# Attention on one core: the product with v one and a half key steps behind the scores, in pieces of half, whole, half

## The chip, the cores and the metric

The kernel runs on one core of a Trainium2 chip. A core has a matrix engine (TensorE, PE in the profile; its loads of the stationary operand are shown as PEld), a vector engine (VectorE, DVE), a scalar engine for activations (ScalarE, ACT), a general engine (GpSimd, POOL) and an engine that issues transfers (SyncE, SP). Each works through its own list of instructions in order; semaphores make one wait for another. The metric is the device time in microseconds (us); three runs of the kernel before the change gave 2307.34, 2310.35 and 2310.27, median 2310.27.

## The reference

One transformer block on 2048 tokens of width 576, in float32: modulation by a condition vector, attention with 32 heads of width 18 that share one key and one value head, and a channel MLP of width 4608, each behind a LayerNorm.

```
h = layernorm(x) * (1 + ca) + sa
q = h @ wq   (32 heads of 18);  k = h @ wk;  v = h @ wv   (one head of 18)
p = softmax(q k^T * 18**-0.5);  o = p v
x = x + ga * (o @ wo)
h = layernorm(x) * (1 + cb) + sb
x = x + gb * (gelu(layernorm(h) @ w1 + b1) @ w2 + b2)
```

## The kernel before

The program has three stages: projections (to about 138 us), attention (to about 1431 us), MLP. The order of instructions on each engine is the order in which the Python code issues them; there is no scheduler.

Attention goes through 32 **quads**. A quad is one block of 512 queries and four heads. For each quad the 2048 keys are taken in 16 **key steps** of 128. In one key step the scores of the four heads are four matmuls (`st_mm`, L790), each of 64 rows of the array, with the keys stationary and 512 queries streaming; heads of group g = 0 use the upper half of the array's rows and those of g = 1 the lower half, so that two neighbouring matmuls of different g run at the same time. Each result fills one of the four PSUM banks called psB, and ScalarE turns it into exponentials (L792), one instruction a bank, in a quarter of an SBUF tile P; three such tiles exist. The product with v (`pv_mm`, L779) takes a whole tile P as moving operand, with v (32 columns) stationary, in four column groups for the four heads, and adds all 16 key steps up in the single PSUM bank psC. A call for all 512 queries is a whole, for 256 a half.

The rows of the queries carry the negated maximum of their scores, so the scores come out with it subtracted. These maxima are computed one quad and two loop steps ahead: in every loop step, for two lots of 128 queries (g = 0 and 1), the scores against all 2048 keys are formed again in pieces of 512 keys. They are `m` (`mx_mm`, L313, into one of three banks psM, reduced by VectorE, L812), six a loop step; `x` (L800, a psB bank), the difference of two key blocks, of which ScalarE takes the relu (L803); and `r` (L313, psM), which VectorE combines with that relu (L810), so that eight pieces cost seven VectorE results.

A **loop step** `d` (there are 256, eight a quad) covers two key steps and follows a written list of tokens, MIX: `s0`/`s1` a score matmul of group 0 or 1, `m0`/`m1`, `x1`, `r1` as above, `H` a half product and `P` a whole one. The last ten steps have no maxima to compute and follow PLAIN. Behind a finished key step `between(n, kc)` issues what is due by the number kc of the key step: at 12 the last reductions of the maxima (L346, L347), at 13 their transpose on TensorE (L351), ScalarE's and VectorE's halves of the negated value (L353, L354) and four transfers into the queries' rows; one piece of every finished quad's normalisation (`post_quad`: copy of psC by ScalarE, L610; at 1 a transpose of 32x32 blocks on VectorE, L614; at 2 a reciprocal, L617; at 4 a second transpose, L622; at 5 another copy); at odd kc one piece of other work (first weights, then for each block of 512 queries the product with wo, L591, and for the first two blocks the second LayerNorm, with L138 to L143 on VectorE); and on GpSimd the preparation of the MLP's weights.

Of the kernel before, what the change touches and what calls it, by code (L numbers as in the profile page):

```python
# [14 lines left out]
S, D, H, DH, F = 2048, 576, 32, 18, 4608  # L15
# [5 lines left out]
NQT = NB * NQ  # L21
# [9 lines left out]
def block_kernel(ctx: ExitStack, tc, x, wqkv, wo, w1, b1, w2, b2, c, wmod, ident_in, out):  # L31
# [20 lines left out]
    def psC(): return PS["t"].tile([128, 512], F32, name="psC", bufs=1)  # L52

    open_ps("1", 3)
    def big(): return per.tile([128, 10, 512], F32R, name="big", bufs=3)
# [244 lines left out]
    def load_q(n):  # L300
        tb, qd = divmod(n, NQ)
        if n not in QST:
            new_q(n)
        q = QST[n]
        for g in range(2):
            for r in range(3):
                src = qscr[tb, r // 2, 4 * DH * qd:4 * DH * (qd + 1), :]
                src = src.rearrange("(p g d) t -> g d p t", p=2, g=2)[g]
                sy.dma_start(q[64 * g + DH * r:64 * g + DH * (r + 1)].bitcast(F32), src)
# [30 lines left out]
    def smax_fin1(n):  # L340
        m = MR[n] = pa.tile([128, 16], F32, name="mxf", bufs=2)
        mm = MX.pop(n)
        if n == 0:
            ve.tensor_reduce(m, mm, axis=AX.X, op=ALU.max)
        else:
            ve.tensor_reduce(m[:, :8], mm[:, :8, :], axis=AX.X, op=ALU.max)  # L346
            ve.tensor_reduce(m[:, 8:], mm[:, 8:, :3], axis=AX.X, op=ALU.max)  # L347

    def smax_fin2(n):
        p = psB()  # L350
        pe.transpose(p[:16, :128], MR.pop(n), ident)  # L351
        ms = pa.tile([16, 2, 128], F32R, name="ms")
        ac.activation(ms[:, 0], p[:16, :128], AF.Copy, scale=-1.0)  # L353
        ve.scalar_tensor_tensor(ms[:, 1], p[:16, :128], -1.0, ms[:, 0].bitcast(F32), op0=ALU.mult, op1=ALU.subtract)  # L354
        for g in range(2):
            for s in range(2):
                r = 64 * g + R3 + s
                sy.dma_start(QST[n][r:r + 1].rearrange("o p (t c) -> o (p t) c", c=128).bitcast(F32),
                             ms[8 * g:8 * (g + 1), s].bitcast(F32))
# [80 lines left out]
    for tb in range(NB):  # L440
# [3 lines left out]
        for i, m in enumerate((4, 0, 1, 2, 3)):  # L444
            np_ = NPART[tb][i]
# [29 lines left out]
            if tb < 2:  # L475
                for _ in range(NSTAT[tb][i]):
                    ln1_stats(*stats.popleft())
                for _ in range(NAPPLY[tb][i]):
                    b, t = applies.popleft()
# [269 lines left out]


    SH = 2
    MIX = "x1 m0 m0 s1 s0 r1 H s1 s0 m1 s0 H m0 s1 m1 s0 s1 m0 P".split()
    PLAIN = "s0 s1 s0 s1 P s0 s1 s0 s1 P".split()
    P, PVt = {}, {}
    posts = []
    fill = deque([late_weights()])
# [12 lines left out]
                units[8 * (n - 1) + u - SH] = (n, u)  # L769
    assert min(units) == 0 and u1 == 2 * SH  # L770

    def pv_mm(n, kc, h0, h1):

        if kc == 0 and h0 == 0:
            PVt[n] = psC()
        t = P.pop((n, kc)) if h1 == 4 else P[n, kc]
        cs = slice(128 * h0, 128 * h1)
        for j in range(4):
            pe.matmul(PVt[n][32 * j:32 * (j + 1), cs], V[:, kc, :], t[:, j, cs],  # L779
                      start=(kc == 0 and h0 == 0), stop=(kc == 15), skip_group_check=True)  # L780
        if kc == 15 and h1 == 4:
            gen = post_quad(n, PVt.pop(n))
            next(gen)
            posts.append(gen)
# [29 lines left out]
    def between(n, kc):  # L814

        if kc == 12 and n + 1 < NQT:
            smax_fin1(n + 1)
        if kc == 13 and n + 1 < NQT:
            smax_fin2(n + 1)
        for gen in list(posts):  # L820
            if next(gen, 0) == 0:
                posts.remove(gen)
        if kc == 1 and n >= 1 and n + 2 < NQT:
            load_q(n + 2)
        if kc == 8 and n % NQ == 0 and n:
            fill.append(wo_block(n // NQ - 1))
            if n // NQ - 1 < 2:
                fill.append(ln2_block(n // NQ - 1))
        if kc % 2:
            step(fill)  # L830
        if n > 2 and kc not in (11, 12):
            step(prep)
        if kc == 8 and n == NQT - 1:
            while prep:
                step(prep)
            W1["r"] = per.tile([128, 40, 128], F32R, name="w1a", tag="big", bufs=3)
            load_w1(0, " ".join(OPS) + " tails")

    for d in range(8 * NQT):
        n, kd = divmod(d, 8)  # L840
        if kd == 0 and n % NQ == 0:
            ATT[n // NQ] = big()
        un = units.get(d)
        ns, nm, np_ = [0, 0], [0, 0], 0
        for tok in MIX if un else PLAIN:
            if tok in "PH":
                s, h0 = 2 * d + np_ // 4, np_ % 4
                np_ += 4 if tok == "P" else 2
                if s:
                    pv_mm(*divmod(s - 1, 16), h0, (np_ - 1) % 4 + 1)  # L850
                if np_ % 4 == 0:
                    between(n, s % 16)
                continue
            g = int(tok[1])
            if tok[0] == "s":
                st_mm(n, 2 * kd + ns[g] // 2, g, ns[g] % 2)
                ns[g] += 1
            else:
                mx_mm(*un, tok[0], g, nm[g])
                nm[g] += tok[0] == "m"  # L860
    pv_mm(NQT - 1, 15, 0, 4)
    while fill:
        step(fill)
    a2.__exit__(None, None, None)
# [465 lines left out]
```

## Time and profile before

| | |
|---|---|
| median of three runs | 2310.27 us |
| profiled execution | 2309.73 us |
| its span, first to last instruction | 2307.9 us |
| granted TensorE clock | 0.999 |
| TensorE busy | 2277.1 us (99%) |
| VectorE busy | 1721.7 us (75%) |
| ScalarE busy | 1495.4 us (65%) |
| GpSimd busy | 1272.1 us (55%) |

In a timeline each row gives the start in us from the span's start, the time that it covers, the engine, the line in the kernel, the operation, the tile written and the tiles read, the shape, and how many instructions in a row it stands for. A bracket gives the time for which the engine was idle before it and what ended the wait. Matmuls are pipelined: the next may start before the last one's shown end, so distances of starts say more than durations. The four matmuls of a product in the code are eight in the trace (x8).

### The profile page before, as it was taken

Reading aid. Unit: us, or ns where it says so; the run is one execution under the profiler, and the core shown is the slowest. Engines: PE = TensorE matmul, PEld = TensorE weight load, DVE = VectorE, ACT = ScalarE, POOL = GpSimd, SP = SyncE. Lnnn points to the kernel's source line nnn. Section 1 sums busy time; section 2 is a strip of 40 time slices with the busy share of each in tenths; the row PEclk is TensorE's granted clock in tenths of the full one; section 3 lists DMA queues with packets and bytes.
Section 4 is the critical chain, followed back from the end, with each engine's and each line's share of the span. In section 5 each row is a group of like instructions: output and inputs, shape, how many; then the busy total and the mean of one; then the engine's idle time right before and its main releaser. Section 6 shows DMA issues by size and latency. Waiting matters only on the chain.

```text
span 2307.9 us, 44339 instructions
## 1 busy us (share of the span) xinstructions
PE 2277.1 (99%) x16390; PEld 1421.0 (62%) x16390; DVE 1721.7 (75%) x3068; ACT 1495.4 (65%) x2879; POOL 1272.1 (55%) x1489
## 2 busy tenths in 40 slices
PE   8999999999999999999999999999999999999999
PEld 6643434354444454444444344899999999899898
DVE  6589999989999979999889992444444456666665
ACT  5558999979999969999889998322222232222221
POOL 6501534335555525656334332488888767677776
PEclk9999999999999999999999999999999999999999
DMA  6422122212222212212122222445445446666664
GB/s 221 139 71 74 49 78 78 84 45 73 80 78 67 88 50 70 84 61 80 64 73 76 72 82 78 152 158 173 145 154 175 151 157 197 180 181 180 178 184 125
DMA packets 145625, 259.91 MB, mean 113 GB/s; under 512 B 15755, under 2 KB 56587, under 8 KB 145409
## 3 DMA queue, kind: packets, MB, share of 16 engines
q1 hardware_dynamic: 145409, 257.07, 35.0%
q8 instruction: 130, 2.13, 0.4%
q14 instruction: 86, 0.70, 0.1%
HBM read 156.11 MB, written 92.01 MB: 108 GB/s over the span
## 4 chain that ended last, share of the span: by engine, by line
PE 90%; ACT 3%; DVE 1%; POOL 0%; issue 0%; POOLq 0%
PE psC L779 22%; PE psB L1006 18%; PE psB L790 12%; PE psA L1117 10%; PE psM L313 10%; PE psA L1086 8%; PE psB L800 4%; PE psB L591 2%; ACT P L792 2%; ACT O L610 1%; PE psA L591 1%; PE psB L150 0%; PE psB L242 0%; PE psB L197 0%; ACT xc L803 0%
## 5 line engine op out<-in xcount | busy, mean ns | idle before, releaser
L792 ACT ACTIVATE P<-psB 128x512 f32<-128x512 f32 x2048 | 1048.5, 621 | 3.5 <-PE psB L790 2.5
L812 DVE TENSOR_REDUCE mx<-psM 128x1 f32<-128x512 f32 x1476 | 943.4, 682 | 48.1 <-PE psM L313 20.3
L779 PE MATMUL psC<-P,V 128*32 128x256 f32 (+1 forms) x6056 | 598.7, 467 | 13.4 <-ACT O L610 13.4
L790 PE MATMUL psB<-qst,KS 64*128 64x512 f32 x2048 | 597.8, 434 | 0.0
L313 PE MATMUL psM<-KS,qst 64*128 64x512 f32 x1722 | 596.8, 432 | 0.2
L790 PEld LDWEIGHTS psB<-qst,KS 64*128 64x128 f32 x2048 | 301.4, 184 | 167.3 <-issue 71.7
L1006 PE MATMUL psB<-ops,w1a 128*128 128x512 f32 x1512 | 390.5, 396 | 0.0
L313 PEld LDWEIGHTS psM<-KS,qst 64*128 64x128 f32 x1722 | 284.9, 185 | 123.3 <-DVE mx L810 90.2
L1006 PEld LDWEIGHTS psB<-ops,w1a 128*128 128x128 f32 x1512 | 271.6, 188 | 47.7
L779 PEld LDWEIGHTS psC<-P,V 128*32 128x32 f32 x6056 | 119.6, 108 | 234.1 <-issue 209.5
L1117 PE MATMUL psA<-w2s,big 128*128 128x288 f32 x1488 | 255.4, 295 | 0.0
L1021 ACT ACTIVATE yr<-psB,b1t 128x512 f32<-128x512 f32 x72 | 49.6, 689 | 287.4 <-PE psB L1006 147.4
L1117 PEld LDWEIGHTS psA<-w2s,big 128*128 128x128 f32 x1488 | 221.3, 188 | 6.7
L803 ACT ACTIVATE xc<-psB 128x512 f32<-128x512 f32 x246 | 149.0, 606 | 90.1 <-PE psM L313 75.0
L1121 DVE TENSOR_TENSOR XT<-psA,XT 128x576 f32<-128x576 f32 x152 | 114.3, 752 | 121.4 <-PE psA L1117 121.3
L1021 ACT ACTIVATE gx<-psB,b1t 128x512 f32<-128x512 f32 x72 | 49.6, 688 | 223.9 <-PE psB L1006 75.4
L130 POOL MEMSET qst<- 32x1024 f32 x62 | 58.6, 945 | 200.1 <-issue 73.7
L810 DVE CUSTOM_DVE_ANT_0 xc<-psM,xc 128x512 f32<-128x512 f32 x246 | 167.2, 680 | 0.3 <-ACT xc L803 0.2
L1092 DVE TENSOR_TENSOR XT<-psA,XT 128x576 f32<-128x576 f32 x170 | 128.8, 758 | 32.7 <-PE psA L1086 23.4
L800 PEld LDWEIGHTS psB<-KD,qst 64*128 64x128 f32 x246 | 45.1, 183 | 159.2 <-ACT P L792 109.4
L1025 POOL TENSOR_TENSOR big<-gx,big 128x512 fp32r<-128x512 f32 x72 | 94.7, 1316 | 62.6 <-ACT big L1024 45.7
L800 PE MATMUL psB<-KD,qst 64*128 64x512 f32 x246 | 122.2, 497 | 0.0
(193 smaller groups left out, 2977.0 us busy)
## 6 DMA issues: line engine op xcount, KB each, us to landing
w1a<-w1scr SPq DMA_DIRECT2D x154, 256.0 KB
w1scr<-w1a SPq DMA_DIRECT2D x98, 256.0 KB
w2scr<-r SPq DMA_DIRECT2D x72, 288.0 KB
w2sum<-r SPq DMA_DIRECT2D x68, 288.0 KB
w2s<-w2sum SPq DMA_DIRECT2D x68, 288.0 KB
w2s<-w2scr SPq DMA_DIRECT2D x29, 576.0 KB
qst<-qscr SPq DMA_DIRECT2D x192, 72.0 KB
w2s<-w2scr SPq DMA_DIRECT2D x34, 288.0 KB
```

The lines of the kernel that those rows point to most:

```text
L313: pe.matmul(o, QST[n][64 * g:64 * g + 64, p, 128 * qt:128 * (qt + 1)], KS[64 * g:64 * g + 64, 512 * kb:512 * (kb + 1)], start=True, stop=True)
L779: pe.matmul(PVt[n][32 * j:32 * (j + 1), cs], V[:, kc, :], t[:, j, cs], start=(kc == 0 and h0 == 0), stop=(kc == 15), skip_group_check=True)
L790: pe.matmul(t, KS[64 * g:64 * g + 64, 128 * kc:128 * (kc + 1)], QST[n][64 * g:64 * g + 64, i, :], start=True, stop=True)
L792: ac.activation(P[n, kc][:, 2 * i + g, :], t, AF.Exp, scale=SCALE)
L800: pe.matmul(t, QST[n][64 * g:64 * g + 64, p, 128 * qt:128 * (qt + 1)], KD1[64 * g:64 * g + 64, :], start=True, stop=True)
L803: ac.activation(XC[-1], t, AF.Relu)
L810: ve.tensor_tensor_reduce(c, t, c, 1.0, -3.0e38, ALU.add, ALU.max, o)
L812: ve.tensor_reduce(o, t, axis=AX.X, op=ALU.max)
L1006: pe.matmul(o, x, y, start=(first and i == 0), stop=(i == len(terms) - 1), skip_group_check=True)
L1086: pe.matmul(p[:, i, :288], x[:, ts_], W2S[k][:, y], start=(bool(first) and q == 0), stop=(q == 2), skip_group_check=True)
L1092: ve.tensor_tensor(o, p[:, :, :288], o, op=ALU.add)
L1117: pe.matmul(p[:, nn, :288], x, y, start=(q == 0), stop=(q == len(terms) - 1))
```

## The change

The two lists of tokens are written anew. Before, a loop step did half, half, whole: the two halves finished the last key step of the loop step before, and the whole was this loop step's first key step. Now the pieces are half, whole, half, and the product runs three half key steps behind (`LAG = 3`): the first half finishes the key step before the last, the whole takes the last one, and the second half begins this loop step's first key step. `pv_mm` counts half key steps. The scores and maxima are spread anew over the spaces between. `between` is called behind the whole for the even key step and behind the second half for the odd one; before, behind the second half and the whole. Two calls behind the loop finish the last key steps. PLAIN gets three pieces a step where it had two.

```diff
-    MIX = "x1 m0 m0 s1 s0 r1 H s1 s0 m1 s0 H m0 s1 m1 s0 s1 m0 P".split()
-    PLAIN = "s0 s1 s0 s1 P s0 s1 s0 s1 P".split()
+    MIX = "x1 s0 s1 H m1 s0 s1 m0 m1 s0 P m0 s1 s0 s1 m0 r1 H m0".split()
+    PLAIN = "s0 s1 H s0 s1 s0 s1 P s0 s1 H".split()
+    LAG = 3
...
-    def pv_mm(n, kc, h0, h1):
-        if kc == 0 and h0 == 0:
+    def pv_mm(i, k):
+        n, kc, h = i // 32, i // 2 % 16, i % 2
+        if kc == 0 and h == 0:
             PVt[n] = psC()
-        t = P.pop((n, kc)) if h1 == 4 else P[n, kc]
-        cs = slice(128 * h0, 128 * h1)
+        end = h + k == 2
+        t = P.pop((n, kc)) if end else P[n, kc]
+        cs = slice(256 * h, 256 * (h + k))
...
-        ns, nm, np_ = [0, 0], [0, 0], 0
+        ns, nm, i = [0, 0], [0, 0], 4 * d - LAG
         for tok in MIX if un else PLAIN:
             if tok in "PH":
-                s, h0 = 2 * d + np_ // 4, np_ % 4
-                np_ += 4 if tok == "P" else 2
-                if s:
-                    pv_mm(*divmod(s - 1, 16), h0, (np_ - 1) % 4 + 1)
-                if np_ % 4 == 0:
-                    between(n, s % 16)
+                k = 2 if tok == "P" else 1
+                if i >= 0:
+                    pv_mm(i, k)
+                i += k
+                if tok == "P":
+                    between(n, 2 * kd)
+                elif i % 4 == 1:
+                    between(n, 2 * kd + 1)
                 continue
...
-    pv_mm(NQT - 1, 15, 0, 4)
+    pv_mm(32 * NQT - LAG, 1)
+    pv_mm(32 * NQT - 2, 2)
```

The change moves instructions in nearly every step; the first place is TensorE at the border of two quads. The numbers behind a name tell buffers apart, so a new number at psC is the new quad's sum. Before, from the last half of the old quad to the next step's x:

```order
L779 MATMUL psC_4194<-P_4675,V_81 32x256 x4
L313 MATMUL psM_4755<-KS_80,qst_4201 128x512
L790 MATMUL psB_4758<-qst_3628,KS_80 128x512
L313 MATMUL psM_4761<-KS_80,qst_4201 128x512
L790 MATMUL psB_4764<-qst_3628,KS_80 128x512
L790 MATMUL psB_4767<-qst_3628,KS_80 128x512
L313 MATMUL psM_4770<-KS_80,qst_4201 128x512
L779 MATMUL psC_4773<-P_4720,V_81 32x512 x4
L800 MATMUL psB_4792<-KD1_82,qst_4201 128x512
```

Now, from the whole that ends the old quad (L782 is the same line, three further down; L793 and L803 likewise):

```order
L782 MATMUL psC_4191<-P_4672,V_81 32x512 x4
L313 MATMUL psM_4752<-KS_80,qst_4198 128x512
L793 MATMUL psB_4755<-qst_3625,KS_80 128x512
L793 MATMUL psB_4758<-qst_3625,KS_80 128x512
L793 MATMUL psB_4761<-qst_3625,KS_80 128x512
L313 MATMUL psM_4764<-KS_80,qst_4198 128x512
L313 MATMUL psM_4767<-KS_80,qst_4198 128x512
L782 MATMUL psC_4770<-P_4714,V_81 32x256 x4
L313 MATMUL psM_4789<-KS_80,qst_4198 128x512
L803 MATMUL psB_4792<-KD1_82,qst_4198 128x512
```

In both the old quad's last product and the new quad's first stand six matmuls apart; the new quad now opens with a half at the end of the step instead of a whole, r1 (the second of the two L313 in a row) stands just ahead of it, and one m0 has moved between it and x1.

The second place is VectorE behind the same border, with the transposes of the old quad's sums. Before:

```order
L812 TENSOR_REDUCE mx_3417<-psM 128x1 x4
L614 STREAM_TRANSPOSE T<-O 128x512
L812 TENSOR_REDUCE mx_3417<-psM 128x1 x2
L810 ISA xc,mx_3417<-psM,xc 128x512
L810 ISA mx_3417 128x1
L812 TENSOR_REDUCE mx_3417<-psM 128x1
L617 RECIPROCAL R<-T 128x16
L812 TENSOR_REDUCE mx_3417<-psM 128x1 x5
```

Now (L815 is the same line as L812 before, L813 as L810):

```order
L815 TENSOR_REDUCE mx_3428<-psM 128x1 x6
L813 ISA xc,mx_3428<-psM,xc 128x512
L813 ISA mx_3428 128x1
L614 STREAM_TRANSPOSE T<-O 128x512
L815 TENSOR_REDUCE mx_3428<-psM 128x1 x4
L617 RECIPROCAL R<-T 128x16
L815 TENSOR_REDUCE mx_3428<-psM 128x1 x2
L813 ISA xc,mx_3428<-psM,xc 128x512
```

L614 stood four maxima behind one r1 (L810) and two ahead of the next; now it stands directly behind an r1 (L813), with all six maxima of a step between it and the next. L617 stood one maximum behind r1 and now stands four behind L614.

More of the change, by code (lines that the diff above doesn't have):

```diff
@@ L770, in block_kernel @@
     assert min(units) == 0 and u1 == 2 * SH
-    def pv_mm(n, kc, h0, h1):
-        if kc == 0 and h0 == 0:
+    def pv_mm(i, k):
+        n, kc, h = i // 32, i // 2 % 16, i % 2
+        if kc == 0 and h == 0:
             PVt[n] = psC()
-        t = P.pop((n, kc)) if h1 == 4 else P[n, kc]
-        cs = slice(128 * h0, 128 * h1)
+        end = h + k == 2
+        t = P.pop((n, kc)) if end else P[n, kc]
+        cs = slice(256 * h, 256 * (h + k))
         for j in range(4):
             pe.matmul(PVt[n][32 * j:32 * (j + 1), cs], V[:, kc, :], t[:, j, cs],
-                      start=(kc == 0 and h0 == 0), stop=(kc == 15), skip_group_check=True)
-        if kc == 15 and h1 == 4:
+                      start=(kc == 0 and h == 0), stop=(kc == 15), skip_group_check=True)
+        if kc == 15 and end:
             gen = post_quad(n, PVt.pop(n))
```

## The prediction

> **What bounds the kernel now.** I read the page's busy times first, then the windows by stage, then the timeline of TensorE over one quad, and last those of VectorE and ScalarE over the same stretch. Each row gives busy time, mean nanoseconds of one instruction and idle time before it.
>
> ```profile
> PE 2277.1 (99%) x16390; PEld 1421.0 (62%) x16390; DVE 1721.7 (75%) x3068; ACT 1495.4 (65%) x2879; POOL 1272.1 (55%) x1489
> ...
> L792 ACT ACTIVATE P<-psB 128x512 f32<-128x512 f32 x2048 | 1048.5, 621 | 3.5 <-PE psB L790 2.5
> L812 DVE TENSOR_REDUCE mx<-psM 128x1 f32<-128x512 f32 x1476 | 943.4, 682 | 48.1 <-PE psM L313 20.3
> ```
>
> The shares of the whole span mislead here. In the window of the attention loop (columns: length, then PE, PEld, DVE, ACT, POOL) three engines are close to full:
>
> ```profile
> 138.00:1388.00 1250.00, 1236.42 (x10307) 533.26 (x10306) 1153.96 (x2238) 1159.53 (x2317) 541.78 (x669) 1.00 0.22 71
> ```
>
> DVE and ACT are busy 92 and 93%. TensorE's 99% includes waits, so I take its starts instead. One quad, steps opening with L800:
>
> ```profile
> 334.12 0.28 PE L351 MATMUL psB<-ident,mxf 128*16 128x128 f32 x1
> 334.32 0.49 PE L800 MATMUL psB<-KD,qst 64*128 64x512 f32 x1
> ...
> 337.03 0.50 PE L313 MATMUL psM<-KS,qst 64*128 64x512 f32 x1
> ...
> 337.60 0.39 PE L313 MATMUL psM<-KS,qst 64*128 64x512 f32 x1
> 337.93 1.06 PE L779 MATMUL psC<-P,V 128*32 128x512 f32 x8
> 338.92 0.50 PE L800 MATMUL psB<-KD,qst 64*128 64x512 f32 x1
> ...
> 339.49 0.39 PE L790 MATMUL psB<-qst,KS 64*128 64x512 f32 x1
> 339.51 0.49 PE L313 MATMUL psM<-KS,qst 64*128 64x512 f32 x1
> 339.93 0.64 PE L779 MATMUL psC<-P,V 128*32 128x256 f32 x8
> 340.50 0.50 PE L790 MATMUL psB<-qst,KS 64*128 64x512 f32 x2
> ...
> 341.73 0.49 PE L313 MATMUL psM<-KS,qst 64*128 64x512 f32 x1
> ...
> 342.30 0.39 PE L790 MATMUL psB<-qst,KS 64*128 64x512 f32 x1
> 343.15 1.06 PE L779 MATMUL psC<-P,V 128*32 128x512 f32 x8 [0.45 <-ACT O L610]
> 344.15 0.49 PE L800 MATMUL psB<-KD,qst 64*128 64x512 f32 x1
> ...
> 348.73 0.50 PE L800 MATMUL psB<-KD,qst 64*128 64x512 f32 x1
> ...
> 353.44 0.49 PE L800 MATMUL psB<-KD,qst 64*128 64x512 f32 x1
> ...
> 358.36 0.50 PE L800 MATMUL psB<-KD,qst 64*128 64x512 f32 x1
> ...
> 372.70 0.50 PE L800 MATMUL psB<-KD,qst 64*128 64x512 f32 x1
> ```
>
> Scores and maxima start in pairs, one on each half of the array's rows. Three pairs up to a product take 337.93-337.03 = 0.90, two pairs with a half product 341.73-340.50 = 1.23, a half 340.50-339.93 = 0.57 (so the two pairs 0.66), a whole 338.92-337.93 = 0.99. A step has pairs 3, 2, 3 and half, half, whole: 0.90+0.57+0.66+0.57+0.90+0.99 = 4.59, and 344.15 to 348.73 is 4.58. That is the floor; eight steps of it with the transpose of the maxima (L351, 334.32-334.12 = 0.20) make 36.9, and the quad from 334.32 to 372.70 took 38.38. So about **1.5 us of waits per quad** are all that an order can win or lose. I number the quad's steps 0 to 7; step 0 starts at 338.92 and the quoted stretch opens with a step 7. The waits are of two kinds.
>
> First, in step 0 the new quad's first product should start 0.33 after 342.30, at 342.63, and starts at 343.15: **0.52**, for the copy of the old sums out of the only psC bank. Second, r1 starts at 339.51 instead of 339.49 and the product 0.42 instead of 0.33 behind it: about **0.12**, in step 2 (348.73 to 353.44, 4.71), 0.34 in step 3 (to 358.36, 4.92), and again 0.12 each in steps 4 to 6 (14.34 in all, less 0.20). Steps 1 and 7 have none. Sum 0.52+0.12+0.12+0.34+0.36 = 1.46. Who holds r1 is seen on VectorE:
>
> ```profile
> 334.73 0.28 DVE L354 SCALAR_TENSOR_TENSOR ms<-psB,ms 16x128 fp32r<-16x128 f32 x1
> 334.94 1.27 DVE L812 TENSOR_REDUCE mx<-psM 128x1 f32<-128x512 f32 x2
> ...
> 337.57 3.21 DVE L812 TENSOR_REDUCE mx<-psM 128x1 f32<-128x512 f32 x5 [0.15 <-PE psM L313]
> ...
> 342.26 1.89 DVE L812 TENSOR_REDUCE mx<-psM 128x1 f32<-128x512 f32 x3 [0.27 <-PE psB L790]
> 344.06 0.70 DVE L614 STREAM_TRANSPOSE T<-O 128x512 f32<-128x512 f32 x1
> 344.71 1.29 DVE L812 TENSOR_REDUCE mx<-psM 128x1 f32<-128x512 f32 x2
> ```
>
> Three reductions in a row take 1.89 with 0.69 for the last, so one each 0.60. psM has three banks: r1 needs the bank of the third map before it. The first of those three starts on PE at 337.03, on DVE at 337.57, and the third's result is there at 337.57+1.89 = 339.46, 0.03 before r1's turn: too late for its weights to be loaded ahead, hence the 0.12. Whatever DVE does besides lands on r1.
>
> By the Trainium skill ("VectorE: DVE Perf Modes", The DRAIN you can't avoid) the next VectorE operation does not start until the pipeline of the last is empty. Seven results of 682 ns would then need 4.77 a step, DVE would set every step, and the change could move nothing. The row at 342.26 and the step of 4.58 disagree, so this case gets no chance; the sum goes by 0.60.
>
> **The change part by part.** No matmul, exponential or reduction is added or removed in the mixed steps. Pieces become half, whole, half with pairs 2 (the last m0 with the next x1, then s0 s1), 3 and 3 before them: 0.66+0.57+0.90+0.99+0.90+0.57 = 4.59. The floor stays.
>
> *The copy of psC.* ScalarE in step 0 (start, time for all):
>
> ```profile
> 339.45 0.60 ACT L803 ACTIVATE xc<-psB 128x512 f32<-128x512 f32 x1
> 339.95 2.66 ACT L792 ACTIVATE P<-psB 128x512 f32<-128x512 f32 x5
> 342.48 0.62 ACT L610 ACTIVATE O<-psC 128x512 f32<-128x512 f32 x1
> 342.95 1.61 ACT L792 ACTIVATE P<-psB 128x512 f32<-128x512 f32 x3
> ```
>
> The copy stands behind one relu and five exponentials, 3.56 after the step's start, and its result comes at 4.18. In the new order it again stands behind one relu and five exponentials. Back to back these take 0.50 and 0.48 each (1.61 for three, 0.65 of it the last), so the copy starts at 0.53+0.50+5x0.48 = 3.43 at best, 3.56 at worst, and ends at 4.05 to 4.18. The first product is now the last half of the step: 0.66+0.57+0.90+0.99+0.90 = 4.02 after x1, 4.14 if r1 has waited. The wait shrinks from 0.52 to about 0.03. **-0.5 per quad.**
>
> *r1's usual wait.* In both orders three maxima stand ahead of r1 with the same work between the first of them and r1: three pairs, the whole product, two pairs, 0.90+0.99+0.57 = 2.46. So it stays at 0.12, not below.
>
> *What the copy's wait had covered.* Seven results take 7x0.60 = 4.20 of a step of 4.71; 0.5 is free. L614 comes right behind r1's and the last maxima's work and takes 344.71-344.06 = 0.65. Before, it fell into the 0.52 in which TensorE stood still, and step 1 ran at the floor. Now TensorE does not stand. Followed through: the three maps behind the whole product start on DVE at 3.12+0.54 = 3.66, 4.26 and 4.86; L614 takes 5.46 to 6.11; the next m0 is done at 6.71, and m1, whose map is ready at 4.71+1.23+0.54 = 6.48, starts 0.23 late. r1 of step 1 waits 0.12+0.23 = 0.35 where it waited 0. **+0.35.**
>
> The second transpose (L622, the same operation) comes behind the first three maps of step 2 and pushes the next by about 0.5; before, the idle time ahead of the last three maps (0.27 in the row at 342.26) took part of it and it cost 0.34-0.12 = 0.22 in step 3. Now the bank of the first of those maps is wanted by the first pair of the next step: map ready on DVE 3.57+0.65 = 4.22, read by 4.91, wanted about 0.1 earlier than 4.71: 0.3. **+0.1.**
>
> Step 7 was free of waits because the transpose L351 (0.20) let DVE catch up; now the two small closing reductions stand behind the third map and L354 (0.21, from 334.73 and 334.94) behind r1, where the next m0 is due, and r1's 0.12 is back. The last exponentials of a step come nearer to the next (the last pair of scores 4.59-0.66-0.57-0.90-0.99-0.34 = 1.13 before x1 instead of 338.92-337.60 = 1.32), and with L353 or the copy in ScalarE's queue one of the four psB banks comes free 0.1 late in steps 1 and 7. **+0.3** (0 to 0.5).
>
> The four transfers of the negated maxima hang on L353 and L354 as well. SyncE issued them so:
>
> ```profile
> 334.72 2.82 SPq L358 DMA_DIRECT2D qst<-ms  x4
> ```
>
> The issue ends at 337.54, and the first scores that need them start at 338.92+0.34 = 339.26 without a wait. L353 may come 0.2 later behind a busier ScalarE; a step 7 that is longer by 0.2 gives that back. Taken as 0, at most +0.2.
>
> Per plain quad: -0.5+0.35+0.1+0.3 = **+0.25**; bounds -0.5 (every new wait absent) and +0.6.
>
> *Where other work runs.* Counts of L800 by window:
>
> ```profile
> 295.90:449.40 153.50, 15.83 (x32) 5.85 (x32) 1.00 0.25 78
> 576.60:685.30 108.70, 10.92 (x22) 4.02 (x22) 1.00 0.24 74
> 802.40:857.20 54.80, 3.97 (x8) 1.46 (x8) 1.00 0.20 62
> ```
>
> Plain steps take 153.5/32 = 4.80, steps with the second LayerNorm 4.94, with wo 6.85. There are 24 of wo (three blocks of eight) and 90 of LayerNorm (two blocks of four tiles of 11, and 2), of 245 mixed ones; 131, 16.4 quads, are left.
>
> The groups of VectorE in the second of these windows show what comes on top:
>
> ```profile
> L142 DVE BATCH_NORM_STATS2 bst<-XT 128x6 f32<-128x288 f32 x2 | 0.9, 450 | 0.0
> ```
>
> In the 11.3 LayerNorm quads DVE gets four of these a tile besides, behind the same r1, with no standstill to take them: I put the loss at twice the plain one, +0.5 (bounds -0.5, as plain, and +1.0). In the wo steps TensorE is the longer by over 2 us; the copy's wait goes and L614 hides under wo's matmuls: three times -0.5.
>
> *The last ten steps* have no maxima and one more piece each. ScalarE sets them, as its groups from 1387.9 to 1428.6 show:
>
> ```profile
> L792 ACT ACTIVATE P<-psB 128x512 f32<-128x512 f32 x79 | 40.2, 628 | 0.6 <-PE psB L790 0.2
> ```
>
> 80x0.48 = 38.4 of 40.7 us. Two more changes of piece a step at 0.10 each (0.33 into a product, 337.60 to 337.93, against 339.49-338.92-0.34 = 0.23 between pairs) hide under that; between -1.5 and +1, taken as 0. By the Trainium skill ("TensorEngine Tiling (Array Packing)", Key Properties) a change of tiling mode drains TensorE; the same 0.10 is what the trace shows of it, and charged in full it would be +2.
>
> **Sum:** 16.4x0.25 + 11.3x0.5 - 3x0.5 = 4.1+5.7-1.5 = **+8.3**. The profiled execution took 2309.7 (span 2307.9), the median run 2310.3; I forecast 2318.5 for the median.
>
> **The rivals.**
> *A, the copy's wait simply goes* (faster): L614 and L622 fit into the 0.5 that DVE has free per step, r1 stays at 0.12. For it: the free time is nearly as long as L614's 0.65. Against: it lies in two pieces, 0.37 and 0.1. Price: -0.5 in 31 quads, 2295. It decides if L614's push stays under 0.1.
> *B, gain and loss cancel* (no change): L614 costs the 0.35, but step 7 and psB nothing. 27.7 quads by -0.05 and -1.5: 2307 to 2311.
> *C, psB becomes the bound* (clearly slower): exponentials end nearer to x1, and the first pair of scores waits for a bank in every step, not in two. At the 0.10 that an unprepared start costs, in 221 steps without wo: +22, 2332 or more with the rest. Against: ScalarE has 0.28 free in 4.59 (0.50+8x0.48 = 4.34).
>
> **How the numbers follow.** This kernel's measurement tells 0.2%, 4.6 us, from no change. Forecast 0.50 (its own range 2315 to 2325), A 0.19, B 0.21, C 0.10. Faster is A with the lower edge of B, 0.21; same is B and the forecast's lower edge, 0.25; slower the rest, 0.54. 2299 to 2331 leaves out about half of A and of C and holds the rest.
>
> **What would show it.** Right: step 0 near 4.7 with no idle left at psC; steps 1 and 2 near 5.0; step 7 near 4.8; the quad near 38.6. Wrong: step 1 at 4.6 to 4.7 (A), or step 7 at the floor (B), or scores late in every step (C). If r1's product follows within 0.33 throughout, the equality of 2.46 has failed, and with it the sign.

## The result and the profile after

| | before | after |
|---|---|---|
| median of five runs, us | 2309.77 (2307.34 to 2310.35) | 2323.36 (2321.95 to 2325.24) |
| ratio after to before | | 1.006, 95% interval 1.0049 to 1.0071 |
| span of the profiled execution, us | 2307.9 | 2321.1 |
| first x to last x, us | 138.5 to 1383.2 | 139.0 to 1395.1 |
| last x to the next product with wo, us | 48.1 | 49.4 |

The change makes the kernel slower by 13.6 us. The forecast was 2318.5, range 2299 to 2331, with slower as the likeliest case. Almost all of the loss lies in the 245 steps from the first x to the last: 11.4 of the span's 13.2 us.

The page of the kernel after, its busy times and two groups (busy time, mean ns of one, idle time before them and what ended it):

```profile
PE 2293.2 (99%) x16478; PEld 1450.0 (62%) x16478; DVE 1721.3 (74%) x3068; ACT 1498.3 (65%) x2879; POOL 1274.5 (55%) x1489
...
L782 PE MATMUL psC<-P,V 128*32 128x256 f32 (+1 forms) x6144 | 599.9, 462 | 1.0 <-ACT O L610 1.0
L313 PEld LDWEIGHTS psM<-KS,qst 64*128 64x128 f32 x1722 | 289.0, 184 | 452.6 <-DVE mx L815 327.5
```

The same two groups on the page of the kernel before:

```profile
L779 PE MATMUL psC<-P,V 128*32 128x256 f32 (+1 forms) x6056 | 598.7, 467 | 13.4 <-ACT O L610 13.4
...
L313 PEld LDWEIGHTS psM<-KS,qst 64*128 64x128 f32 x1722 | 284.9, 185 | 123.3 <-DVE mx L810 90.2
```

The product's idle time behind the copy of psC went from 13.4 to 1.0 us: that wait is gone, but for one in the last ten steps:

```profile
1413.12 0.64 PE L782 MATMUL psC<-P,V 128*32 128x256 f32 x8 [0.97 <-ACT O L610]
```

The weight loads of the maxima, which are let go when VectorE has read a psM bank, are idle for 452.6 us instead of 123.3. Most of that overlaps matmuls that run anyway, so it is no sum of lost time; *a_border*, a kernel further down whose steps take as long as before, still has 410.4. It says that the load is now ready, and held, at more of the 1722 places. The three engines beside TensorE work as long as before.

The distance from one x to the next is the length of a step. Means over the plain quads, the quads with LayerNorm work and those with wo:

| step | 0 | 1 | 2 | 3 | 4 | 5 | 6 | 7 | quad |
|---|---|---|---|---|---|---|---|---|---|
| before, plain | 5.23 | 4.59 | 4.70 | 4.92 | 4.70 | 4.71 | 4.92 | 4.59 | 38.36 |
| after, plain | 4.72 | 4.97 | 4.90 | 4.80 | 4.70 | 4.70 | 4.91 | 4.87 | 38.58 |
| before, LayerNorm | 5.14 | 4.81 | 4.81 | 5.08 | 4.89 | 4.79 | 4.95 | 4.97 | 39.44 |
| after, LayerNorm | 4.80 | 5.26 | 5.08 | 4.94 | 4.96 | 4.88 | 5.02 | 5.09 | 40.03 |
| before, wo | 7.32 | 6.77 | 6.77 | 6.77 | 6.89 | 6.77 | 6.80 | 6.78 | 54.87 |
| after, wo | 6.92 | 6.88 | 6.90 | 6.88 | 6.90 | 6.89 | 6.90 | 6.88 | 55.15 |

TensorE's timeline after, from a step 7 (x at 335.49) to the end of step 1 (x at 350.05); columns as in the prediction:

```profile
335.49 0.51 PE L803 MATMUL psB<-KD,qst 64*128 64x512 f32 x1
335.83 0.56 PE L793 MATMUL psB<-qst,KS 64*128 64x512 f32 x2
336.32 0.64 PE L782 MATMUL psC<-P,V 128*32 128x256 f32 x8
...
339.34 0.52 PE L313 MATMUL psM<-KS,qst 64*128 64x512 f32 x2
339.78 0.64 PE L782 MATMUL psC<-P,V 128*32 128x256 f32 x8
...
340.36 0.50 PE L803 MATMUL psB<-KD,qst 64*128 64x512 f32 x1
...
344.05 0.50 PE L313 MATMUL psM<-KS,qst 64*128 64x512 f32 x2
344.51 0.64 PE L782 MATMUL psC<-P,V 128*32 128x256 f32 x8
...
345.08 0.49 PE L803 MATMUL psB<-KD,qst 64*128 64x512 f32 x1
345.41 0.57 PE L793 MATMUL psB<-qst,KS 64*128 64x512 f32 x2
345.91 0.64 PE L782 MATMUL psC<-P,V 128*32 128x256 f32 x8
...
346.81 0.84 PE L313 MATMUL psM<-KS,qst 64*128 64x512 f32 x2
347.17 0.49 PE L793 MATMUL psB<-qst,KS 64*128 64x512 f32 x1
347.59 1.07 PE L782 MATMUL psC<-P,V 128*32 128x512 f32 x8
...
350.05 0.50 PE L803 MATMUL psB<-KD,qst 64*128 64x512 f32 x1
```

Step 0 (340.36 to 345.08, 4.72) opens the new quad's sum at 344.51, 0.46 after r1's pair (344.05) where 0.33 is the floor: only r1's usual 0.1 is left. Step 1 (345.08 to 350.05, 4.97) loses 0.38. The scores behind x need 0.50 (345.41 to 345.91) instead of 0.33, for a bank of psB, and the maxima ahead of the whole need 0.78 (346.81 to 347.59) instead of 0.57, for a bank of psM. Step 7 (335.49 to 340.36, 4.87) has two waits as well: the scores 0.49 (335.83 to 336.32), and r1's pair 0.44 (339.34 to 339.78). VectorE and ScalarE in steps 0 and 1:

```profile
342.11 3.19 DVE L815 TENSOR_REDUCE mx<-psM 128x1 f32<-128x512 f32 x5 [0.31 <-PE psB L793]
345.22 0.68 DVE L813 CUSTOM_DVE_ANT_0 xc<-psM,xc 128x512 f32<-128x512 f32 x1
...
345.83 0.71 DVE L614 STREAM_TRANSPOSE T<-O 128x512 f32<-128x512 f32 x1
346.46 2.45 DVE L815 TENSOR_REDUCE mx<-psM 128x1 f32<-128x512 f32 x4
```

```profile
341.41 2.55 ACT L795 ACTIVATE P<-psB 128x512 f32<-128x512 f32 x5
343.80 0.65 ACT L610 ACTIVATE O<-psC 128x512 f32<-128x512 f32 x1
344.28 1.65 ACT L795 ACTIVATE P<-psB 128x512 f32<-128x512 f32 x3
```

The copy starts 3.44 into step 0 and is done before the product's turn. L614 stands behind r1 as the order said, and the next reduction cannot start before 346.46, while TensorE no longer stands still. The copy itself also pushes three exponentials by half a microsecond, which the scores of step 1 see.

### The profile page after: what moved, and what is told of

Read it like the earlier page. It is cut to its first block, busy times and chain, and to the rows that moved or that the text cites. A ratio compares the mean times of both kernels' runs of the same rounds, so it can differ in the third digit from the quotient of the medians.

```text
span 2321.1 us, 44539 instructions
## 1 busy us (share of the span) xinstructions
PE 2293.2 (99%) x16478; PEld 1450.0 (62%) x16478; DVE 1721.3 (74%) x3068; ACT 1498.3 (65%) x2879; POOL 1274.5 (55%) x1489
## 4 chain that ended last, share of the span: by engine, by line
PE 91%; DVE 6%; ACT 1%; POOL 1%; issue 0%; DMA 0%; ACTq 0%; POOLq 0%
PE psC L782 21%; PE psB L1012 18%; PE psM L313 18%; PE psA L1123 10%; PE psA L1092 8%; PE psB L793 8%; DVE mx L815 3%; PE psB L591 2%; PE psB L242 2%; PE psB L150 1%; PE psA L313 1%; PE psB L197 1%; PE psA L591 1%; DVE O L622 1%; ACT P L795 1%
## 5 line engine op out<-in xcount | busy, mean ns | idle before, releaser
L795 ACT ACTIVATE P<-psB 128x512 f32<-128x512 f32 x2048 | 1063.3, 623 | 39.3 <-PE psB L793 23.6
L815 DVE TENSOR_REDUCE mx<-psM 128x1 f32<-128x512 f32 x1476 | 941.8, 682 | 76.7 <-PE psB L793 56.9
L313 PE MATMUL psM<-KS,qst 64*128 64x512 f32 x1722 | 611.3, 450 | 8.1 <-DVE mx L815 5.2
L782 PE MATMUL psC<-P,V 128*32 128x256 f32 (+1 forms) x6144 | 599.9, 462 | 1.0 <-ACT O L610 1.0
L313 PEld LDWEIGHTS psM<-KS,qst 64*128 64x128 f32 x1722 | 289.0, 184 | 452.6 <-DVE mx L815 327.5
L793 PE MATMUL psB<-qst,KS 64*128 64x512 f32 x2048 | 568.8, 427 | 1.4 <-ACT xc L806 0.9
L793 PEld LDWEIGHTS psB<-qst,KS 64*128 64x128 f32 x2048 | 267.8, 185 | 33.9 <-ACT P L795 18.4
L782 PEld LDWEIGHTS psC<-P,V 128*32 128x32 f32 x6144 | 121.2, 108 | 211.9 <-issue 201.5
L1123 PEld LDWEIGHTS psA<-w2s,big 128*128 128x128 f32 x1488 | 221.3, 188 | 6.7
L813 DVE CUSTOM_DVE_ANT_0 xc<-psM,xc 128x512 f32<-128x512 f32 x246 | 167.2, 680 | 0.0
L803 PE MATMUL psB<-KD,qst 64*128 64x512 f32 x246 | 122.3, 497 | 0.0
L1092 PEld LDWEIGHTS psA<-w2s,big 128*128 128x128 f32 x816 | 115.4, 188 | 6.2
```

The lines of the kernel that those rows point to most:

```text
L313: pe.matmul(o, QST[n][64 * g:64 * g + 64, p, 128 * qt:128 * (qt + 1)], KS[64 * g:64 * g + 64, 512 * kb:512 * (kb + 1)], start=True, stop=True)
L793: pe.matmul(t, KS[64 * g:64 * g + 64, 128 * kc:128 * (kc + 1)], QST[n][64 * g:64 * g + 64, i, :], start=True, stop=True)
L795: ac.activation(P[n, kc][:, 2 * i + g, :], t, AF.Exp, scale=SCALE)
L803: pe.matmul(t, QST[n][64 * g:64 * g + 64, p, 128 * qt:128 * (qt + 1)], KD1[64 * g:64 * g + 64, :], start=True, stop=True)
L813: ve.tensor_tensor_reduce(c, t, c, 1.0, -3.0e38, ALU.add, ALU.max, o)
L815: ve.tensor_reduce(o, t, axis=AX.X, op=ALU.max)
```

## The experiments

The theory: the copy's wait had covered L614 and L622, and the loss is what comes out from under it. The rivals: the trade is even and the loss lies elsewhere; or nothing was covered. Six kernels bear on the trade, two on where the other work stands, four on what holds the waits that are left. Each ratio is against the kernel before, timed beside it on the same chip; two kernels that were not timed together are compared by their distances from it. The lengths of steps are the finer measure: the medians also hold one-off differences of 1 to 5 us, at the start of the maxima (TensorE's clock is granted at half for 3.4 us there in the kernel after, for 6.8 before and in a_tr, for 10.2 in a_both, and not at all in b_both) and at one place near 230 us, of which more below. Both places lie in the first 24 steps. So the tables also give the 221 steps from the 25th on, as their sum in the profiled execution against that of the kernel before (1121.1 us).

### Copy and transposes on the kernel before: cut one, the other, both

*b_copy* cuts the copy of psC to 32 of 512 columns, *b_tr* cuts the two transposes likewise, *b_both* cuts all three. A tile that is then written only in part (O for the copy, T for the transposes) is allocated once and filled with ones.

```diff
-        ac.activation(O, PV, AF.Copy)
+        ac.activation(O[:, :32], PV[:, :32], AF.Copy)
...
-        ve.transpose(T.rearrange("p a b -> p (a b)"), O)
+        ve.transpose(T[:, 0, :], O[:, :32])
...
-        ve.transpose(O, T.rearrange("p a b -> p (a b)"))
+        ve.transpose(O[:, :32], T[:, 0, :])
```

> The kernel before with the copy of psC cut from 512 columns to 32 (the other sums are left out of the output, so the result is not the attention's). If the copy's wait is what gave VectorE the time for L614: step 0 falls from 5.23 to 4.75 to 4.9, step 1 rises from 4.59 to 4.8 or more, and the time falls by 2 to 5 us only. If the waits are independent: step 0 falls, step 1 stays at 4.59, and the time falls by 0.45 x 31 = 14 us.

> The kernel before with both 32x32 transposes (L614, L622) cut from 512 columns to 32, so the output is not the attention's. If L614 was covered: step 0 stays at 5.2, step 1 at 4.59, only step 3 and the LayerNorm steps get shorter, 4 to 7 us in all. If each transposition costs its 0.6 us: 2 x 0.5 x 31 = 31 us less.

> The kernel before with both cuts (copy and transposes). If the copy's wait and L614 cover each other, the gain is larger than the sum of the two single ones: 12 to 16 us against 2 to 5 and 4 to 7. If they are independent it is their sum.

| | median us | ratio (95%) | steps 0 to 3, plain | quad | from the 25th step on |
|---|---|---|---|---|---|
| before | 2308.87 | | 5.23 4.59 4.70 4.92 | 38.36 | 0 |
| b_copy | 2305.14 | 0.9983 (0.9973 to 0.9992) | 4.82 4.89 4.59 5.04 | 38.25 | -3.5 |
| b_tr | 2305.20 | 0.9984 (0.9974 to 0.9993) | 5.22 4.58 4.69 4.90 | 38.30 | -4.5 |
| b_both | 2294.63 | 0.9934 (0.9919 to 0.9949) | 4.82 4.59 4.70 4.90 | 37.89 | -15.0 |

TensorE in b_copy, where x is L808, the scores L798 and the product L787; step 1 runs from 342.34 to 347.24:

```profile
342.34 0.50 PE L808 MATMUL psB<-KD,qst 64*128 64x512 f32 x1
...
345.62 0.38 PE L798 MATMUL psB<-qst,KS 64*128 64x512 f32 x1
345.81 0.50 PE L313 MATMUL psM<-KS,qst 64*128 64x512 f32 x1
346.24 1.06 PE L787 MATMUL psC<-P,V 128*32 128x512 f32 x8
347.24 0.49 PE L808 MATMUL psB<-KD,qst 64*128 64x512 f32 x1
```

The same step in b_both, from 343.10 to 347.69:

```profile
343.10 0.50 PE L808 MATMUL psB<-KD,qst 64*128 64x512 f32 x1
...
346.37 0.39 PE L798 MATMUL psB<-qst,KS 64*128 64x512 f32 x1
346.69 1.07 PE L787 MATMUL psC<-P,V 128*32 128x512 f32 x8
347.69 0.49 PE L808 MATMUL psB<-KD,qst 64*128 64x512 f32 x1
```

With the copy short and nothing moved, step 0 wins 0.41 and step 1 at once loses 0.30: a map of the maxima starts 0.19 after its partner (345.81 against 345.62) and the product 0.43 after the map. With the transposes short as well, the pair and the product follow as they should and step 1 is back at 4.59. Cutting one wins 3.7 us, cutting the other 3.7, cutting both 14.2, almost twice the sum; from the 25th step on it is 3.5, 4.5 and 15.0. So the copy's wait and the transposes cover each other; in step 1 that is L614. That is shown on the kernel before, without the change's order. One point of b_tr missed: step 3 should have become shorter and did not (see below), and 3.7 lies just under the 4 to 7 expected.

### The same on the kernel after

*a_tr*, *a_copy* and *a_both* are the same three cuts in the changed kernel.

> The changed kernel with both 32x32 transposes cut to 32 columns (output not the attention's). If they hold r1 and the next m0: step 1 falls from 4.97 to about 4.75, step 2 from 4.90 to 4.70, and the time by 9 to 14 us, about twice what the same cut gives the kernel before. If psB and ScalarE hold these steps: both stay above 4.85 and the time falls by under 4 us.

> The changed kernel with the copy of psC cut from 512 columns to 32 (output not the attention's). If nobody waits for the copy any more and only VectorE holds step 1: under 2 us less, step 1 stays at 4.97. If ScalarE's queue is a bound beside it: step 1 falls by 0.1 to 0.2 and the time by 3 to 6 us.

> The changed kernel with the copy and both transposes cut to 32 columns (output not the attention's). The cut transposes alone gave 4.5 us of the 9 to 14 expected, with step 3 grown from 4.80 to 5.00. If ScalarE's lag took over there: step 1 falls to 4.70, and the gain is clearly more than that of the two single cuts together, 8 to 13 us. If something else holds step 3: the sum of the two, 5 to 8 us, and step 3 stays at 5.0.

| | median us | ratio (95%) | steps 0 to 3, plain | quad | from the 25th step on |
|---|---|---|---|---|---|
| after | 2323.36 | 1.0060 (1.0049 to 1.0071) | 4.72 4.97 4.90 4.80 | 38.58 | +10.8 |
| a_copy | 2321.54 | 1.0062 (1.0047 to 1.0077) | 4.70 4.99 4.91 4.80 | 38.58 | +10.3 |
| a_tr | 2318.86 | 1.0039 (1.0024 to 1.0054) | 4.72 4.87 4.70 5.00 | 38.49 | +5.8 |
| a_both | 2313.37 | 1.0023 (1.0013 to 1.0034) | 4.70 4.70 4.70 5.00 | 38.27 | +1.2 |

Cutting the copy alone moves no step by over 0.02: nobody waits for it any more. Cutting the transposes was expected to win 9 to 14 us and won 3.6 (from 13.6 over the kernel before to 10.0), or 5.0 from the 25th step on. Step 1 kept 0.17 over the usual 4.70, which goes only when the copy is cut too: the copy's push on the exponentials, which had been hidden behind VectorE's. Step 2 won 0.20 and step 3 gave it all back, from 4.80 to 5.00. Of what was expected of a_both, the first branch holds for step 1 and for the time (8.4 us, against 0.2 and 3.6 for the single cuts), the second for step 3. And a_both stands 5.2 us over the kernel before where b_both stands 14.2 under it: with both sides of the trade taken out, the change loses 19 us instead of 13.6 (16.2 instead of 10.8 from the 25th step on). The trade alone does not make the loss, and the theory falls in that part.

### Who holds step 3

Behind the second transpose ScalarE copies the normalised sums (L629). *a_three* is a_both with 480 of the 512 columns of that copy moved to GpSimd.

```diff
-        ac.activation(os[:, 0], O, AF.Copy)
+        ac.activation(os[:, 0, :32], O[:, :32], AF.Copy)
+        po.tensor_copy(os[:, 0, 32:], O[:, 32:])
```

> The changed kernel with the copy of psC and both transposes cut to 32 columns and all but 32 columns of the second copy (os, L629) given to GpSimd (output not the attention's). If ScalarE's 0.52 for os holds the scores in step 3: step 3 falls from 5.00 to about 4.7 and the time by 5 to 8 us against the two cuts without it (2313). If not: step 3 stays at 5.0.

Measured 2304.57, ratio 0.9985 (0.9976 to 0.9994); plain steps 4.70 4.70 4.70 4.70 4.70 4.71 4.91 4.87. That is 8.8 us under a_both by the distances from the kernel before, and 6.8 from the 25th step on, where 5 to 8 was expected. Step 3, from 5.00 to 4.70, was ScalarE's. In the kernel before, the prediction had put r1's wait of 0.34 in step 3 down to L622. In b_tr, where L622 is short, the step takes 4.90 all the same; TensorE in it:

```profile
353.36 0.50 PE L808 MATMUL psB<-KD,qst 64*128 64x512 f32 x1
...
354.38 0.64 PE L787 MATMUL psC<-P,V 128*32 128x256 f32 x8
...
355.28 0.39 PE L313 MATMUL psM<-KS,qst 64*128 64x512 f32 x1
355.36 0.49 PE L798 MATMUL psB<-qst,KS 64*128 64x512 f32 x1
355.79 0.64 PE L787 MATMUL psC<-P,V 128*32 128x256 f32 x8
...
358.27 0.49 PE L808 MATMUL psB<-KD,qst 64*128 64x512 f32 x1
```

r1 is back at its usual 0.12 (the product at 354.38, 1.02 after x, as the 339.93-338.92 = 1.01 of an ordinary step), and the scores wait instead: the pair at 355.28 comes apart by 0.08 and the product follows at 355.79, 0.51 after it instead of 0.33. ScalarE's row ahead of that step in b_tr:

```profile
353.66 0.67 ACT L637 ACTIVATE os<-O 128x512 fp32r<-128x512 f32 x1
```

Two waits, each hiding the other, stood in step 3 as well. That the second is ScalarE's is read from these rows; the cut of L629 was run on the changed kernel alone.

### Where the other work stands

In the kernel before, the odd call of `between`, which issues L351, a tile of wo or of LayerNorm work, stands behind the whole product, between the three maxima and r1. In the changed kernel it stands behind the second half, after r1. *a_border* puts it back behind the whole in the changed kernel; *b_border* puts it behind the second half in the kernel before. In both the even call goes to the head of the step.

```diff
+        between(n, 2 * kd)
         for tok in MIX if un else PLAIN:
...
                 if tok == "P":
-                    between(n, 2 * kd)
-                elif i % 4 == 1:
                     between(n, 2 * kd + 1)
```

```diff
+        between(n, 2 * kd)
         for tok in MIX if un else PLAIN:
...
-                if np_ % 4 == 0:
-                    between(n, s % 16)
+                if np_ == 4:
+                    between(n, 2 * kd + 1)
```

> The changed kernel with the calls between key steps moved: the odd one, with all of TensorE's other work, from behind the last half to behind the whole (so between the three maxima and r1), the even one to the start of the step. If r1's 0.12 in wo steps and in step 7 comes from this work no longer lying between the three maxima and r1: the seven wo steps other than step 0 go from 6.88 back to 6.77, step 7 from 4.87 to 4.7, step 6 from 4.91 to 4.80, and the time falls by 7 to 11 us. If it does not matter where the work lies: within 2 us of the changed kernel.

> The kernel before with the calls between key steps moved the other way: the odd one, with TensorE's other work, from behind the whole (between the three maxima and r1) to behind the second half, the even one to the start of the step. Pieces and order of scores and maxima stay. If the place of this work against r1 is what counts: wo steps go from 6.77 to 6.88, step 7 from 4.59 to 4.8 or more, step 6 rises too, and the time rises by 10 to 18 us, about what the change cost. If not: within 3 us of the kernel before.

| pieces | odd call | | median us | ratio (95%) | quad, plain | quad, LayerNorm | step with wo | from the 25th step on |
|---|---|---|---|---|---|---|---|---|
| old | behind the whole | before | 2308.15 | | 38.36 | 39.44 | 6.77 to 6.80, step 0 7.32 | 0 |
| new | behind the whole | a_border | 2312.97 | 1.0021 (1.0012 to 1.0031) | 38.29 | 39.40 | 6.79 to 6.80 | -0.9 |
| old | behind the half | b_border | 2328.10 | 1.0090 (1.0074 to 1.0105) | 38.93 | 40.04 | 6.88 to 6.91 | +15.2 |
| new | behind the half | after | 2323.36 | 1.0060 (1.0049 to 1.0071) | 38.58 | 40.03 | 6.88 to 6.92 | +10.8 |

(In a_border one step with wo in eight takes 7.29, the last of a block; step 4 of the wo quads before takes 6.89.) The rows of a step with wo show it: the pair with r1 and the loads of its weights (PEld), the half product, and wo (L591) behind it, in the kernel after:

```profile
819.04 0.42 PEld L313 LDWEIGHTS psM<-KS,qst 64*128 64x128 f32 x2
819.26 0.51 PE L313 MATMUL psM<-KS,qst 64*128 64x512 f32 x2
819.70 0.64 PE L782 MATMUL psC<-P,V 128*32 128x256 f32 x8
820.27 2.25 PE L591 MATMUL psB<-wos,big 126*128 126x288 f32 x15
```

and in a_border, where wo stands ahead of r1:

```profile
821.89 2.23 PE L591 MATMUL psB<-wos,big 126*128 126x288 f32 x15
...
824.39 0.18 PEld L313 LDWEIGHTS psM<-KS,qst 64*128 64x128 f32 x2
824.62 0.39 PE L313 MATMUL psM<-KS,qst 64*128 64x512 f32 x2
824.94 0.64 PE L782 MATMUL psC<-P,V 128*32 128x256 f32 x8
```

With 2.2 us of wo between the three maxima and r1, both loads of the pair run together (0.18 in all), 0.23 ahead of the matmuls, and the product follows at 0.32. With wo behind r1 the second load comes only at 819.28, together with its matmul: VectorE reads the bank that r1 needs from 818.54 and begins with the next at 819.23. The product follows at 0.44, although TensorE has just spent 2.2 us on wo a step ago.

The call's place alone decides the length of the LayerNorm quads (39.4 or 40.0) and of the steps with wo (6.8 or 6.9), whichever the pieces. By the medians it is worth 13.6-4.8 = 8.8 us in the new pieces, within the 7 to 11 expected, and 19.9 in the old, where 10 to 18 was expected; from the 25th step on it is 11.7 and 15.2. The call also orders VectorE's LayerNorm work, and these runs do not separate that from TensorE's. One expectation missed: step 6 should have come down to 4.80 with L351 behind the whole, and stayed at 4.89.

By its steps a_border should equal the kernel before; by the median it is 4.8 us over. The 19th step holds the difference: 9.96 us, where the kernels before and after take 4.99 and 5.17. TensorE, ScalarE and GpSimd of a_border there:

```profile
232.77 1.28 PE L793 MATMUL psB<-qst,KS 64*128 64x512 f32 x2 [2.04 <-ACT P L795]
```

```profile
231.55 0.68 ACT L510 ACTIVATE wos<-bigw 128x576 fp32r<-128x576 f32 x1 [2.41 <-POOL bigw L508]
```

```profile
230.12 1.40 POOL L508 TENSOR_TENSOR bigw<-bigw,gab 128x576 f32<-128x576 f32 x1 [8.14 <-DMA bigw<-in_wo]
```

and its windows (length, then PE, PEld, DVE, ACT, POOL, the granted clock, DMA share, GB/s):

```profile
230.20:232.70 2.50, 0.54 (x6) 0.18 (x2) 1.50 (x4) 1.15 (x3) 2.50 (x3) 0.92 0.00 0
232.70:239.30 6.60, 6.53 (x28) 2.52 (x30) 2.54 (x5) 4.60 (x11) 3.93 (x3) 0.51 0.00 0
239.30:245.00 5.70, 5.70 (x52) 2.20 (x48) 4.98 (x10) 5.70 (x12) 3.54 (x3) 1.00 0.06 13
```

The weights of wo land at about 230 us in the kernels before and after too, and GpSimd waits 8.2 and 7.7 us for them there. In a_border, where the call comes earlier in the step, ScalarE reaches L510 before GpSimd has finished, the exponentials queue behind it, TensorE stands still for 2.04 us, and the clock granted to it is 0.51 for the next 6.6. The stall thus costs 4.7 us once (the 19th to the 22nd step: 25.14 against 20.42), at a place that has nothing to do with the order of a quad. b_border has it too (8.47 in the 19th step, 2.7 more over the same four), so some 15 of its 19.9 us are the steps'. A moved call is not the only way to it: b_both, whose calls stand where they stood, has it as well (8.55; ScalarE waits 2.06 for L508 there), and its gain of 14.2 would be larger without it; so has a_r1early below (8.47). What counts is whether ScalarE comes to L510 before the weights have landed and been multiplied.

### The pieces without the rest, and r1's distance

*c_turned* writes the new pieces (half, whole, half, with the lag) into the order of before: r1 stands at the step's end, the even and the odd call where they stood among the maxima (b0, b1; PLAIN gets them too).

```diff
+    MIX = "s0 s1 m0 s1 b0 H s0 m1 s1 m0 s0 m1 P b1 x1 m0 s1 s0 m0 r1 H".split()
...
+            if tok[0] == "b":
+                between(n, 2 * kd + int(tok[1]))
```

> The pieces of the change (half, whole, half, three half steps behind), with the step turned: s0 s1 m0 s1, half, s0 m1 s1 m0 s0 m1, whole, other work, x1 m0 s1 s0 m0 r1, half. Other work lies between the three maxima and r1 and the relu's scores come last. If the change lost by these places and not by its pieces: 15 to 18 us less than the changed kernel, 1 to 6 us less than the kernel before. If the pieces themselves cost: at or above the changed kernel's 2323.

Measured 2311.58, ratio 1.0012 (1.0003 to 1.0022), quad 38.31: 10 us better than the change, but not faster than before, where 1 to 6 us less was expected. One step of 10.93 holds the stall at L510 again, some 6 us; from the 25th step on the kernel is 3.2 us under the one before. It is not quite the order of before: the old quad's last product is now the whole, behind b0, so L614 starts 2.7 us behind the copy (346.86 and 349.56) instead of 1.6 (342.48 and 344.06).

*a_r1early* moves one pair of scores behind r1, so that the work between the three maxima and r1 shrinks by that pair.

```diff
-    MIX = "x1 s0 s1 H m1 s0 s1 m0 m1 s0 P m0 s1 s0 s1 m0 r1 H m0".split()
+    MIX = "x1 s0 s1 H m1 s0 s1 m0 m1 s0 P m0 s1 m0 r1 s0 s1 H m0".split()
```

> The changed kernel with r1 one pair earlier in its group (m0 s1, m0 r1, s0 s1 in place of m0 s1, s0 s1, m0 r1): 2.23 instead of 2.46 between the first of the three maxima and r1. If this distance against VectorE's three results sets r1's wait: it grows by 0.23 in every step, steps 4 and 5 go from 4.70 to about 4.9, and the time rises by 35 to 50 us. If r1 waits for its relu or for the pair's other matmul: within 5 us.

Measured 2354.02, ratio 1.0198 (1.0179 to 1.0217). Steps 0 to 5 all take 4.93. The stretch behind the whole, with r1 in it:

```profile
351.81 0.49 PE L313 MATMUL psM<-KS,qst 64*128 64x512 f32 x1
...
353.04 0.64 PE L782 MATMUL psC<-P,V 128*32 128x256 f32 x8
```

Three pairs take 1.23 there; in the kernel after they take 1.03 (343.48 to the product at 344.51), at the floor 0.90. Steps 4 and 5 grow by 0.23 as expected; steps 1 and 2, which had 0.2 to 0.4 of waits already, do not grow. The sum is 32 us more than the change (by two timed runs), 3.2 of it in the stall at L510; expected were 35 to 50. So r1 does wait for VectorE's three results, and other waits of a step are absorbed in that one.

*a_late* is a_border with the reciprocal one call later, to part it from L614.

```diff
         ve.transpose(T.rearrange("p a b -> p (a b)"), O)
         yield
+        yield
         R = px.tile([128, 16], F32, name="R", bufs=2)
```

> The kernel with the calls moved (2313 us) and one more call between L614 and the reciprocal, so that reciprocal, L622 and os come half a step later, off the three maxima. If VectorE's extra work costs by the place in which it falls: L622 leaves the place behind the three maxima, step 2 falls to 4.7, step 3 rises to 4.9, LayerNorm steps get shorter, and the time falls by 3 to 6 us to about the kernel before. If only its amount counts: within 1.5 us of 2313.

Measured 2309.92, ratio 1.0006 (0.9997 to 1.0015), quad 38.21: 3 us better than a_border, and not to be told from before. Step 2 falls from 4.90 to 4.70, step 3 rises from 4.80 to 4.90. Its 19th step takes 10.14, so it has the stall of 4.9 us as well; from the 25th step on it is 5.2 us under the kernel before. No kernel that computes everything beat the one before. a_late with the first weights' work left at its old calls, and so without the stall, was not tried; 2309.9-4.9 = 2305 is an estimate, not a measurement.

## Why the prediction was right, and where not

- **The floor of 4.59 and the list of waits** held: no mean of a plain step is under 4.58 in any kernel, and b_both runs step 1 at 4.59.
- **The copy of psC**, -0.5: step 0 from 5.23 to 4.72. The copy starts 3.44 into the step, as computed (3.43 to 3.56).
- **What the wait had covered**, +0.35 in step 1: +0.38. The size is right, its place is not: the working had all of it at r1, the trace has 0.17 at the scores behind x and 0.21 at the maxima ahead of the whole. Cutting the transposes alone takes 0.10 off the step, cutting the copy alone nothing, cutting both 0.27: L614 on VectorE and the copy's push on ScalarE stand beside each other, and the working had only the first.
- **L622**, +0.1 in step 2: +0.20 there, and step 3 fell by 0.12 (together +0.08). The reading behind it, that L622 cost step 3 of before 0.22, holds only as long as nothing else stands there: with L622 short (b_tr) the step is as long, for ScalarE's copy L629.
- **Step 7 and psB**, +0.3: +0.28, in the two places named (r1's 0.1 and the scores, 0.16). Plain quads: +0.22 each where +0.25 was forecast, 3.7 us in all against 4.1.
- **r1's usual wait** stayed, as the equality of 2.46 said, and a_r1early shows what a shorter distance costs. By the Trainium skill ("VectorE: DVE Perf Modes", The DRAIN you can't avoid), as the prediction read it, seven results of 682 ns would fill 4.77 a step. The prediction left out that the same section lets an operation that is not held start earlier. Plain steps of 4.70 and five results in a row in 3.19 us (the row at 342.11) agree with the section read whole.
- **LayerNorm quads**, +5.7: measured +6.8. The size is right by luck, the reason was not: "no standstill to take them" speaks of VectorE's load, but cutting the transposes wins the same 0.37 a quad in a_tr (40.03 to 39.66) and in b_tr (39.44 to 39.07). The place of the odd call alone moves these quads between 39.4 and 40.0. Whether that is TensorE's part of the LayerNorm work or VectorE's stays open.
- **The step that failed** is the wo term, -1.5: measured +0.9. The copy's wait did go (step 0, -0.40), but six of the other seven steps grew by about 0.1 each. The prediction counted the matmuls between the three maxima and r1 and found 2.46 in both orders, and did not count what `between` puts there. It saw this once, for the transpose L351 in step 7, and not that wo and the LayerNorm work move out of the same stretch.
- **The last ten steps**, 0 (-1.5 to +1): +1.3, just outside. Most of it is one wait, the 0.97 for the copy of psC at the one border of two quads without maxima (the row at 1413.12); in the kernel before no product waits there. The prediction had ScalarE setting these steps and did not put the copy into them. With 0.5 at the first x the profiled sum is 3.7+6.8+0.9+1.3+0.5 = 13.2 where 4.1+5.7-1.5 = 8.3 was forecast.
- **Rival A** failed by b_copy: without the copy's wait step 1 pays. **Rival B** is the exact picture of steps 0 to 3 (-0.05 a quad together) but not of step 7. **Rival C** did not happen: steps 4 and 5 stay at 4.70.

So the sign came out right for half of its reason. The trade of the copy's wait against VectorE and ScalarE is real and nearly even; the loss itself comes from where the other work was put, of which the forecast had one case under its right name and one under another.

## What to carry to other kernels

A wait on a nearly full machine is also cover: before it is counted as gain, follow what the other engines do inside it, and expect the next wait to stand a few hundred nanoseconds behind (here 3.7, 3.7 and 14.2 us for one, the other and both). When an order is written anew, list what lies between the filling of a ring of buffers and its reuse, the odd jobs included: work that stands there is slack for the consumer, the same work a few instructions later is not. Test order and placement apart, two by two; here that found an effect of 9 to 20 us (12 and 15 without the one-off differences) that the sum had carried under other names.

## What the runs showed of the hardware

- A standstill of TensorE of 2.04 us was followed by 6.6 us at a granted clock of 0.51, and so cost more than twice its length; in b_border the same stretch has 0.74, in the kernels before and after, without the stall, 1.00. Taken to the edges, the clock is at half for 6.8 us in a_border (232.3 to 239.1), a_late and c_turned, where TensorE stood still for 2.04, 2.34 and 3.17; for 3.4 us in b_border, b_both and a_r1early, where it stood for 1.62, 1.66 and 1.83; and not at all in b_tr, where it stood for 0.89. Ten executions of a_border took from 2308.48 us at a mean granted clock of 1.000 to 2316.57 at 0.996. The Trainium skill ("TensorE: Matmul & The Clock Gate", Part 1: The HAM clock gate) has the clock fall to half after an idle window of about 3.4 us and come back after as much work; the fall and the return are seen here, but a shorter gap was enough.
- A weight load that is held can cost more than its wait: in the rows shown the product follows r1's pair at 0.32 to 0.33 when both loads ran ahead and at 0.42 to 0.46 when r1's did not, though r1's own matmul starts only 0.02 late (339.51 for 339.49 before, 819.28 for 819.26 after). 0.1 in each of 220 steps is more than the whole effect here.
- Cutting an operation to a sixteenth does not cut its time so: the transpose of 512 columns takes 0.70 us and that of 32 takes 0.20, the copy from PSUM 0.62 and 0.22. By the two transposes a column costs (0.702-0.202)/480 = 1.04 ns and a fixed part of 0.17 us is left. The Trainium skill ("VectorE: DVE Perf Modes", The TRN2 errata) puts the measured fixed term at about 150 cycles of VectorE's clock, not the 58 of its formula; at the 0.96 GHz of that page this is an estimate of 0.16 us, and the rows agree.
